# First batch of an attention and token-mixer kernel: v loaded as 128 rows, attention ahead of the token products

## The chip, the cores and the metric

The kernel runs on one core of a Trainium2 chip. A core has five engines, each with its own instruction queue that runs in order: TensorE (PE, matrix products, with PEld for the loading of its weights), VectorE (DVE), ScalarE (ACT), GpSimd (POOL) and SyncE (SP), which here issues DMA transfers. The engines wait for each other through semaphores. Data lies in DRAM, in SBUF (128 partitions) and in PSUM (banks of 128 partitions by 512 floats, into which PE writes). The metric is the device time of one execution in microseconds (us).

## The reference

Local attention with block summaries, followed by a token mixer and a channel mixer, all in float32. Batch 4, 8 heads, 768 positions, head dimension 64.

```python
k_sum = k.reshape(B, H, nb, 32, D).max(axis=3)       # nb = 24 blocks
v_sum = v.reshape(B, H, nb, 32, D).mean(axis=3)
scores_l = q @ k.T / sqrt(D)      # kept where |i - j| < 16
scores_s = q @ k_sum.T / sqrt(D) + log(32)
a = softmax([scores_l, scores_s]);  out = a @ [v, v_sum]
...
x = out as (batch, 768, 512)
h = relu(x.T @ w_tok1) @ w_tok2;  u = x + h.T         # token mixer, 256 hidden
y = u + relu(u @ w_ch1) @ w_ch2                       # channel mixer, 1536 hidden
```

## The kernel before

Heads are worked on in pairs, 4 pairs a batch (the text counts pairs 0 to 3 of batch 0). Positions are cut into 12 windows of 64 queries; each sees 96 keys (64 and 16 on either side) and the 24 block summaries, so 120 columns. For that the host lays out k and v as overlapping windows: `kw` holds the 96 keys of each window with room for the 24 summaries, `vw[b, h]` is 96 rows by 12 windows by 64.

Work on one pair of batch 0 runs through these steps. SP loads k, q and the v of two heads (`load_k`, `load_q`, `load_v`). DVE takes the maximum over key blocks and copies it beside the keys (`key_blocks`, L345 and L354). PE computes scores in two groups of windows (`scores`, L462, tiles `sc`), DVE adds the mask and takes the row minimum (L476), ACT takes the exponential (L486, tiles `e`). PE computes the block means of v (`first_means`, L374, tile `vm`), which DVE copies (L394) and POOL spreads into the last 24 rows of the v tile (L381). POOL also copies the raw v into its tile (L320). PE transposes `e` (`turn`, L524, tiles `et`), ACT evacuates that (L535, `eT`), PE computes the weighted sums (`weighted`, L594, `av`), and DVE normalises them into `x` (L602 to L614).

The token products follow: `tok1` (L748) multiplies x of one pair by w_tok1, ACT and DVE split the result in two parts (L729, L734); `tok2` (L828 and L836, tiles `up`) multiplies that by w_tok2 and adds the transposed x, in two halves of the positions (0 and 1), and ACT and DVE split it into `u`. Then come the channel products: for each of 12 slices f of the hidden layer `ch1` (L897, tiles `hp`) and `ch2` (L940, tiles `acc`).

The weights arrive as 64-bit words and are made into floats by `w_tick(i)`: tick 0 to 2 for w_tok1, 3 to 5 for w_tok2, 6 to 29 for the channel weights (tick 10 for the first product of slice 2). One tick is two loads, two ACT steps (L1466, L1472), one POOL step (L1479), two DVE steps (L1484, L1491) and, from tick 3 on, a split on ACT and POOL (L1511, L1517). The second ACT step writes a scratch tile `wp`, which the DVE steps read beside another tile.

What sets the order: nothing is issued where it is written. `add` records each piece of work with its engine, an estimated duration, its reads and writes and a rank; at the end `Plan.write` runs a list scheduler (`_order`), which simulates engines and DMA with the numbers in the code, takes ready work by rank (R_H first, then R_EVAC, R_ATT, R_LATER, R_W, R_BACK) and then by order of recording, and writes each engine's instructions in the order found. The engines then run them in that order, whatever the real times are. A buffer is a slot of a tag: the n-th slot of a tag with m buffers waits for the last user of slot n - m. PSUM banks have the tags mm and att (two banks each) and acc0 to acc3 (one each).

At the start PE does 21 warm-up products on zeros (L1530), while the first k and q are loaded. In batch 0 loads, attention and token products are recorded mixed, in the order of a list `FIRST`. The v tiles of the other batches are loaded as 96 rows as well, and their products are spread among the channel products of the batch before.

Of the kernel before, what the change touches and what calls it, by code (L numbers as in the profile page):

```python
# [76 lines left out]
class Plan:  # L77
    LATE = {"pe": 0.3, "act": 0.15, "dve": 0.15, "pool": 0.2, "sp": 0.0}
    RATE, FIRST, LAND, LANES = 250.0, 370.0, 2.1, 8

# [45 lines left out]
    def _order(self):  # L126
# [10 lines left out]
        queues = {e: [] for e in self.LATE}  # L137
        events, done, dma, lanes = [], [], 0.0, [0.0] * self.LANES

# [63 lines left out]
def tile_attention_mixer(  # L203
# [22 lines left out]
    def sbuf(shape, tag, name, bufs, dtype=F32):  # L226
        return plan.slot(sb, shape, dtype, tag, name, bufs)
# [19 lines left out]
    early = {n: sbuf([P, NT, D], "w2", f"vw_{n}", NF) for n in range(H)}  # L247
    early_k = sbuf([P, NT, NC], "x", "k_2", 2)
    w1_t = [sbuf([P, 2, NC4, P], "w1", f"w1_{f}", NF, F32R) for f in range(NF)]
    w2_t = [sbuf([P, 2, DM], "w2", f"w2_{f}", NF, F32R) for f in range(NF)]  # L250
# [9 lines left out]
        "start": ["att", "att", "acc0", "acc1"],  # L260
        "turned": ["mm", "mm"],
        0: ["att"],
# [13 lines left out]

    def tok_bank(name, late):
        if state["phase"] == "start":
            return bank(name, ["acc0", "acc1", "att", "att"] if late else ["acc3"])
        return bank(name, BANKS[state["phase"]])  # L280
# [13 lines left out]
    def load_q(p):  # L294
        b, hp = divmod(p, NP)
        q_t[p] = sbuf([P, S], "q", f"q_{p}", 2)
        return load(q_t[p], lambda t: t, q[b, hp], 393)
# [6 lines left out]
    def load_v(n):  # L304
# [7 lines left out]
        if b == 0:  # L312
            raw = early[n]
            load(raw, lambda t: t[:WIN], vw[b, h], 295)
            add(
                "pool", 0.1, lambda: nc.gpsimd.memset(slot.t[:NC, :, D:], 1.0),
                writes=[(slot, 2)], rank=R_ATT,
            )
            add(
                "pool", 0.85, lambda: nc.gpsimd.tensor_copy(slot.t[:WIN, :, :D], raw.t[:WIN]),  # L320
                reads=[(raw, 0)], writes=[(slot, 0)], rank=R_ATT,
            )
            return
# [112 lines left out]
    def scores(p, g, behind=()):  # L436
# [53 lines left out]

        for i in range(TT // 2):
            for j in range(2):
                n = 2 * p + j
                den, T = den_t[n], TT // 2 * g + i
                add(
                    "dve", 0.21, lambda n=n, j=j, i=i: lowest(n, j, i), reads=[(tiles[j], 0), ("mask", 0)],
                    writes=[(e, (j, i)), (den, ("min", T))], rank=R_ATT,
                )
                add(
                    "act", 0.39 if p >= NP else 0.29, lambda n=n, j=j, i=i: power(n, j, i), reads=[(den, ("min", T))],  # L500
                    writes=[(e, (j, i)), (den, ("sum", T))], rank=R_ATT,
                )
# [238 lines left out]
    def tok1(b, p):  # L741
        x2, a = x_t[b, p]
        pt = vm_bank

        def products():
# [9 lines left out]
            "pe", 2.8, products, reads=x_keys(b, p) + [(wt1, i) for i in range(3)],  # L755
            writes=[(pt, "t")], rank=R_ATT,
        )
        split_t1(
            b, p, lambda: pt.t[:, :DTOK].rearrange("p (k c) -> p k c", k=2), (pt, "t"), 0.39
        )  # L760
# [662 lines left out]
    def w_tick(i, behind=()):  # L1423
# [12 lines left out]
        for j in range(2):  # L1436
# [91 lines left out]
    def warm_up():  # L1528
        for _ in range(21):
            nc.tensor.matmul(pw.t, lhsT=warm.t[:, :P], rhs=warm.t, start=True, stop=True)  # L1530
# [6 lines left out]
    )  # L1537
    load_v(0)
    load_v(1)
    load_k(1)  # L1540
    load_q(1)
    load_v(2)
    load_v(3)
    load_k(2)
    key_blocks(0)

    tick = 0
    TICKS = {2: 3, 5: 6, 12: 7, 16: 8}
    for s in range(STEPS):
        att_step(0, s)  # L1550
        if s == 1:
            load_q(2)
        while tick < TICKS.get(s, 0):
            w_tick(tick)
            tick += 1
        if s == 1:
            load_v(4)
            load_v(5)
        if s == 4:
            load_k(3)  # L1560
            load_q(3)
        if s == 5:
            load_v(6)
            load_v(7)
        if FIRST[s][0] == "a":
            p = FIRST[s][1]
            tok1(0, p)
            if p:
                tok2(0, 0, p - 1)
    tok2(0, 0, NP - 1)  # L1570
    while tick < 10:
# [149 lines left out]
```

## Time and profile before

| | us |
|---|---|
| median of 3 runs | 568.28 (567.77 to 569.28) |
| the profiled execution | 566.26 |
| its span, first to last instruction | 564.2 |
| PE busy / DVE / ACT / POOL | 548.9 / 335.4 / 267.9 / 263.8 |
| start of the first channel product | 68.75 |
| mean granted PE clock | 0.994 of full speed |

The profile shows one execution. A row of the timeline gives start, duration, engine, source line, operation, output <- inputs, shape and count; in square brackets the idle time ahead of it and what ended it. A row of the waits gives who waited for whom, the total, how often, and the longest. A row of stretches gives the busy time of each engine in that stretch, the granted PE clock, the mean busy share of the 16 DMA engines and the rate that they moved. Busy PE time includes the pipelined end of a product, so the pitch from one start to the next is what a product costs.

### The profile page before, as it was taken

The page shows a single profiled execution, that of the slowest core. Times are in us where ns is not written, and L with a number is a line of the kernel's source. Part 1 is how long each engine was busy: PE and PEld are TensorE (multiplying, and loading weights), DVE is VectorE, ACT ScalarE, POOL GpSimd, SP SyncE. Part 2 cuts the span into 40 slices and gives each one's busy share as a digit, 9 for nine tenths or more (in the row PEclk, how much of TensorE's full clock was granted, in tenths as well). Part 3 has the DMA queues.
Part 4 walks back from the last instruction along what each step waited for, and adds up shares of the span by engine and source line. Part 5 has one row for each costly group of instructions (what it writes and reads, how often), then busy time and mean ns, then how long its engine had stood idle before and what let it go on. Part 6 is the DMA issues. An engine that isn't in the chain of part 4 may idle for free.

```text
span 564.2 us, 12750 instructions
## 1 busy us (share of the span) xinstructions
PE 548.9 (97%) x4629; PEld 485.7 (86%) x4629; DVE 335.4 (59%) x949; ACT 267.9 (47%) x771; POOL 263.8 (47%) x344
## 2 busy tenths in 40 slices
PE   8769999999999999999999999999999999999997
PEld 4658988878989988878799997887789999999997
DVE  4775677866573336456463436445352494899974
ACT  3668698765574334232242314242234253567642
POOL 1653387851133310158896511049879612444111
PEclk9889999999999999999999999999999999999999
DMA  8964478673755017768795606677788673543621
GB/s 268 341 176 130 130 238 264 200 227 106 219 177 177 26 38 198 188 188 231 224 246 174 130 11 192 147 186 211 188 246 241 181 256 116 193 139 95 198 94 65
DMA packets 133774, 99.52 MB, mean 176 GB/s; under 512 B 88272, under 2 KB 112464, under 8 KB 133712
## 3 DMA queue, kind: packets, MB, share of 16 engines
q1 hardware_dynamic: 133568, 98.52, 59.2%
q8 instruction: 36, 0.59, 0.4%
q14 instruction: 26, 0.21, 0.1%
q10 hardware_dynamic: 144, 0.20, 0.1%
HBM read 68.60 MB, written 28.31 MB: 172 GB/s over the span
## 4 chain that ended last, share of the span: by engine, by line
PE 87%; DMA 7%; DVE 2%; ACT 2%; issue 1%; ACTq 0%; DVEq 0%
PE acc L940 26%; PE hp L897 26%; PE up L836 6%; PE t1q L795 5%; PE av L594 4%; DMA vw<-in_vw 3%; PE sc L462 3%; PE pb L1170 3%; PE pa L1170 2%; PE qb L1170 2%; PE qc L1170 2%; PE pc L1170 2%; DMA w<-in_w_tok 2%; PE vm L748 2%; DMA vb<-in_vb 1%; PE qa L1170 1%
## 5 line engine op out<-in xcount | busy, mean ns | idle before, releaser
L940 PE MATMUL acc<-h,w 128*128 128x512 f32 (+1 forms) x864 | 164.0, 339 | 0.0
L897 PE MATMUL hp<-u,w 128*128 128x512 f32 (+1 forms) x864 | 161.8, 337 | 0.0
L897 PEld LDWEIGHTS hp<-u,w 128*128 128x128 f32 x864 | 133.3, 188 | 18.5 <-issue 1.4
L940 PEld LDWEIGHTS acc<-h,w 128*128 128x128 f32 x864 | 132.4, 188 | 19.1 <-ACT h L909 1.4
L486 ACT ACTIVATE e<-e,den 128x120 f32<-128x120 f32 x192 | 70.3, 386 | 53.0 <-DVE den L476 46.0
L909 ACT ACTIVATE h<-hp 128x512 fp32r<-128x512 f32 (+1 forms) x72 | 35.2, 489 | 117.7 <-PE hp L897 116.8
L914 DVE SCALAR_TENSOR_TENSOR h<-hp,h 128x512 fp32r<-128x512 f32 (+1 forms) x72 | 39.8, 553 | 75.1 <-ACT h L909 75.1
L1017 POOL TENSOR_TENSOR s<-s,w 128x256 f32<-128x256 f32 x84 | 62.2, 746 | 5.1
L979 POOL TENSOR_TENSOR ot<-ot,u 128x512 f32<-128x512 f32 (+1 forms) x24 | 23.7, 1014 | 57.5 <-DVE ot L971 27.7
L476 DVE CUSTOM_DVE_ANT_0 e<-sc,mask_sb 128x120 f32<-128x120 f32 x192 | 41.3, 277 | 15.0 <-PE sc L462 12.1
L1517 POOL TENSOR_TENSOR w<-wb,w 128x256 fp32r<-128x256 f32 x48 | 34.6, 740 | 17.0 <-ACT w L1511 16.7
L836 PE MATMUL up<-wt,t 128*128 128x512 f32 (+2 forms) x192 | 39.1, 344 | 0.0
L781 POOL TENSOR_TENSOR xs<-x,xs 128x512 fp32r<-128x512 f32 x18 | 23.2, 1291 | 21.3 <-ACT xs L776 21.3
L445 POOL MEMSET e<- 128x48 f32 x16 | 2.2, 138 | 65.9 <-DMA away<-e 19.6
L836 PEld LDWEIGHTS up<-wt,t 128*128 128x128 f32 x192 | 30.5, 189 | 2.5
L462 PEld LDWEIGHTS sc<-k,q 64*64 64x64 f32 x768 | 20.3, 135 | 12.0 <-issue 8.8
L462 PE MATMUL sc<-k,q 64*64 64x120 f32 x768 | 27.5, 275 | 3.1 <-DMA w<-in_w_tok 1.9
L594 PEld LDWEIGHTS av<-v,eT 120*64 120x64 f32 x768 | 23.9, 138 | 5.5 <-issue 3.1
L795 PE MATMUL t1q<-xs,ws 128*128 128x256 f32 x216 | 28.5, 283 | 0.0
L418 DVE TENSOR_REDUCE vs<-vb 96x8 f32<-96x256 f32 (+1 forms) x40 | 18.2, 458 | 16.8 <-DMA vb<-in_vb 16.7
L345 DVE TENSOR_REDUCE ks<-k 128x24 f32<-128x768 f32 x16 | 15.2, 947 | 21.3 <-DMA k<-in_kw 21.3
L594 PE MATMUL av<-v,eT 120*64 120x64 f32 (+1 forms) x768 | 26.1, 224 | 1.3 <-ACT eT L535 1.2
(128 smaller groups left out, 881.1 us busy)
## 6 DMA issues: line engine op xcount, KB each, us to landing
w<-in_w_ch SPq DMA_DIRECT2D x48, 256.0 KB
k<-in_kw SPq DMA_DIRECT2D x16, 720.0 KB
v<-in_vw SPq DMA_DIRECT2D x24, 288.0 KB
q<-in_q SPq DMA_DIRECT2D x16, 384.0 KB
away<-e SPq DMA_DIRECT2D x16, 384.0 KB
eT<-away SPq DMA_DIRECT2D x64, 96.0 KB
sums<-s SPq DMA_DIRECT2D x24, 256.0 KB
w2d<-w SPq DMA_DIRECT2D x12, 512.0 KB
```

What stands on the lines that cost most here:

```text
L462: nc.tensor.matmul(tiles[j].t[c * QT : (c + 1) * QT, i * NC : (i + 1) * NC], lhsT=qt.t[rows, t * QT : (t + 1) * QT], rhs=kt.t[rows, t, :], ...
L476: nc.vector.tensor_tensor_reduce(out=e.t[:, j, i * P : i * P + NC], in0=tiles[j].t[:, i * NC : (i + 1) * NC], in1=mask_sb[:, mv, :], op0=A ...
L486: nc.scalar.activation(ei, ei, AF.Exp, bias=den_t[n].t[:, 1, T : T + 1], scale=-1.0, accum_out=den_t[n].t[:, 0, T : T + 1] if p >= NP else ...
L594: nc.tensor.matmul(pv[cs, T], lhsT=eT[:NC, T % (TT // 2), cs], rhs=v.t[:NC, 2 * T + c], start=True, stop=True,)
L795: nc.tensor.matmul(pt.t[:, 2 * P * k : 2 * P * (k + 1)], lhsT=ws[:, wp, T, ks], rhs=xs[:, xp, T], start=(c == 0 and k == 0 and T == 0 and ...
L836: nc.tensor.matmul(pt.t[:, :nt], lhsT=t1.t[:, part, ks], rhs=wt2[w].t[:, k, h0 : h0 + nt], start=(far and k == 0 and i == 0), stop=(k == D ...
L897: nc.tensor.matmul(pt.t[:, :nt], lhsT=w1_t[f].t[:, w, c], rhs=us[c].t[:, part], start=(i == 0), stop=(i == len(ops) - 1),)
L909: lambda: nc.scalar.activation(h.t[:, 0], pt.t[:, :nt], AF.Relu),
L914: lambda: nc.vector.scalar_tensor_tensor(out=h.t[:, 1], in0=pt.t[:, :nt], scalar=0.0, in1=h.t[:, 0].bitcast(F32), op0=ALU.max, op1=ALU.sub ...
L940: nc.tensor.matmul(slot.t[:, c0 : c0 + nt], lhsT=w2_t[f].t[:, w, o * P : (o + 1) * P], rhs=h.t[:, part], start=(f == 0 and w == 0 and part ...
L1017: nc.gpsimd.tensor_tensor(out=out_, in0=left, in1=right, op=op)
L1170: nc.tensor.matmul(bank_.t[:, :HS], lhsT=w(i), rhs=x(j), start=first and n == 0, stop=True, skip_group_check=True,)
```

## The change

All of it concerns batch 0. (1) The raw v of a head is loaded as 128 rows instead of 96: the 96 rows of the head and the first 32 of the next one, which nobody reads. The load is of 393 kB instead of 295. (2) The loads come in the order of the pairs, and the weights behind them; q of pairs 2 and 3 gets buffers of its own (tag w1), so that it waits for none. (3) All attention of batch 0 is recorded ahead of the token products, and w_tok1's ticks have the rank of attention, w_tok2's a lower one. (4) Banks: transposes and weighted sums take mm, mm and acc3, the first token products acc0 and acc1 in turn instead of one bank, the second ones att, att and acc2. The scratch tile `wp` of ticks 0 to 5 moves from PSUM (acc3) to SBUF (tag q). (5) 17 warm-up products instead of 21. (6) Within a group of scores all three tiles of one head come ahead of those of the other. (7) The planner's DMA rate and start, and some paddings between slots (`APART`), have other numbers.

```diff
-    RATE, FIRST, LAND, LANES = 250.0, 370.0, 2.1, 8
+    RATE, FIRST, LAND, LANES = 250.0, 390.0, 2.1, 8
...
+    early_q = {p: sbuf([P, S], "w1", f"q_{p}", NF) for p in (2, 3)}
...
-        "turned": ["mm", "mm"],
+        "turned": ["mm", "mm", "acc3"],
...
-    def tok_bank(name, late):
+    def tok_bank(name, first=False):
         if state["phase"] == "start":
-            return bank(name, ["acc0", "acc1", "att", "att"] if late else ["acc3"])
+            return bank(name, ["acc0", "acc1"] if first else ["att", "att", "acc2"])
...
-            load(raw, lambda t: t[:WIN], vw[b, h], 295)
+            rows = vw.rearrange("b h w t d -> (b h w) t d")[WIN * n : WIN * n + P]
+            load(raw, lambda t: t, rows, 393)
...
-        for i in range(TT // 2):
-            for j in range(2):
+        parts = [(j, i) for j in range(2) for i in range(TT // 2)]
+        if p >= NP:
+            parts.sort(key=lambda x: x[1])
+        for j, i in parts:
...
-        pt = vm_bank
+        pt = tok_bank(f"t1p_{b}_{p}", True)
...
-    APART = {"u1": 32, "t1": 48, "w1": 16}
+    APART = {"u1": 32, "u0": 16, "ot": 32, "t1": 32, "w1": 16}
...
-        first, rank = two[0][2] is None, R_ATT if i < 6 else R_W
+        first, rank = two[0][2] is None, R_ATT if i < 3 else R_LATER if i < 6 else R_W
...
-        pb = bank(f"wp_{i}", ["acc3"] if i < 6 else ["acc0", "acc1"] if i < 10 else ["att"])
+        if i < 6:
+            pb = sbuf([P, 512], "q", f"wp_{i}", 2)
+        else:
+            pb = bank(f"wp_{i}", ["acc3"] if i < 10 else ["att"])
...
-        for _ in range(21):
+        for _ in range(17):
...
+    for p in range(NP):
+        if p:
+            load_k(p)
+            load_q(p)
+        load_v(2 * p)
+        load_v(2 * p + 1)
     key_blocks(0)
...
+    for tick in range(6):
+        w_tick(tick)
     for s in range(STEPS):
         att_step(0, s)
...
+    for tick in range(6, 10):
+        w_tick(tick)
+    tick = 10
+    for p in range(NP):
+        tok1(0, p)
+    for p in range(NP):
+        tok2(0, 0, p)
```

The loads on SP, from pair 2's k on. Before (line numbers of the kernel before; a number behind a name only tells tiles of one name apart):

```order
L290 DMA k_127<-in_kw 128x1440
L290 DMA vw_130<-in_vw 96x768
L290 DMA vw_132<-in_vw 96x768
L1440 DMA w_135<-in_w_tok 128x512 x2
L290 DMA q_203<-in_q 128x768
L1440 DMA w_211<-in_w_tok 128x512 x2
L1440 DMA w_251<-in_w_tok 128x512 x2
L290 DMA k_311<-in_kw 128x1440
L1440 DMA w_336<-in_w_tok 128x512 x2
L290 DMA q_374<-in_q 128x768
L290 DMA vw_402<-in_vw 96x768
L290 DMA vw_418<-in_vw 96x768
```

Of the change:

```order
L291 DMA k_123<-in_kw 128x1440
L291 DMA q_127<-in_q 128x768
L291 DMA vw_143<-in_vw 128x768
L291 DMA vw_163<-in_vw 128x768
L291 DMA k_200<-in_kw 128x1440
L291 DMA q_226<-in_q 128x768
L291 DMA vw_242<-in_vw 128x768
L291 DMA vw_263<-in_vw 128x768
L1444 DMA w_287<-in_w_tok 128x512 x2
L1444 DMA w_356<-in_w_tok 128x512 x2
L1444 DMA w_411<-in_w_tok 128x512 x2
```

Eight loads of token weights (w_tok1 and the first of w_tok2) stood ahead of the last two v; now all of attention's loads stand ahead of the first.

ACT, in the changed kernel, between the exponentials of pair 2 (the second group, `e_1_491`) and those of pair 3 (`e_0_583`); `wt_551` is w_tok1, and w_287, w_356 and w_411 are the three pairs of loads of ticks 0, 1 and 2:

```order
L488 ACTIVATE e_1_491<-e_1_491,den_431 128x120 x3
L1473 ACTIVATE wt_551<-w_287 128x512
L1479 ACTIVATE wp_571<-w_287 128x512
L539 ACTIVATE eT_0_577<-et_0_547 120x384
L1473 ACTIVATE wt_551<-w_356 128x512
L539 ACTIVATE eT_0_600<-et_0_579 120x384
L539 ACTIVATE eT_1_619<-et_1_588 120x384
L539 ACTIVATE eT_1_621<-et_1_596 120x384
L1479 ACTIVATE wp_649<-w_356 128x512
L1473 ACTIVATE wt_551<-w_411 128x512
L1479 ACTIVATE wp_662<-w_411 128x512
L488 ACTIVATE e_0_583<-e_0_583,den_584 128x120 x3
```

Before, at the same place (pair 2's second group is `e_1_355`, pair 3's first `e_0_450`, w_tok1 `wt_357`):

```order
L1466 ACTIVATE wt_357<-w_211 128x512
L535 ACTIVATE eT_0_453<-et_0_413 120x384
L486 ACTIVATE e_1_355<-e_1_355,den_287 128x120
L1466 ACTIVATE wt_357<-w_251 128x512
L486 ACTIVATE e_1_355<-e_1_355,den_284 128x120
L486 ACTIVATE e_1_355<-e_1_355,den_287 128x120
L535 ACTIVATE eT_0_487<-et_0_463 120x384
L1472 ACTIVATE wp_499<-w_211 128x512
L486 ACTIVATE e_0_450<-e_0_450,den_451 128x120
```

The steps on w_tok1 were spread among pair 2's exponentials, and the last of them came behind the first of pair 3; now all six stand between pair 2 and pair 3.

PE, in the changed kernel, from pair 2's weighted sums (`av_684`) through the last token product of the first kind, the identity transposes of a second token product and the matmuls of pair 0's:

```order
L598 MATMUL av_684<-v_408,eT_1_621 64x65 x6
L528 MATMUL et_0_706<-identf,e_0_583 120x128 x3
L528 MATMUL et_0_727<-identf,e_0_583 120x128 x3
L752 MATMUL t1p_0_744<-x_0_379,wt_551 128x128 x12
L528 MATMUL et_1_771<-identf,e_1_654 120x128 x3
L528 MATMUL et_1_779<-identf,e_1_654 120x128 x3
L752 MATMUL t1p_1_785<-x_0_379,wt_551 128x128 x12
L598 MATMUL av_817<-v_545,eT_0_722 64x65 x6
...
L598 MATMUL av_834<-v_574,eT_1_800 64x65 x6
L752 MATMUL t1p_2_850<-x_1_717,wt_551 128x128 x12
L752 MATMUL t1p_3_875<-x_1_717,wt_551 128x128 x12
L832 MATMUL up_0_0_908<-identf,x_0_379 128x128 x4
```

Before, the stretch behind pair 2's weighted sums held one more pair's sums of v, both score groups of pair 3 and the first two second token products between these steps; now scores and sums of pair 3 lie ahead of it, the four first token products stand close together, and the second ones follow behind all attention. The token products of pairs 2 and 3 in the second half (`up_1_2`, `up_1_3`), which stood ahead of the first channel product, now follow behind it.

More of the change, by code (lines that the diff above doesn't have):

```diff
@@ L137, in _order @@
         queues = {e: [] for e in self.LATE}
-        events, done, dma, lanes = [], [], 0.0, [0.0] * self.LANES
+        events, done, dma, lanes = [], [], 0.95, [0.0] * self.LANES
         def release(w):
@@ L295, in load_q @@
         b, hp = divmod(p, NP)
-        q_t[p] = sbuf([P, S], "q", f"q_{p}", 2)
+        q_t[p] = early_q[p] if p in early_q else sbuf([P, S], "q", f"q_{p}", 2)
         return load(q_t[p], lambda t: t, q[b, hp], 393)
@@ L755, in tok1 @@
             "pe", 2.8, products, reads=x_keys(b, p) + [(wt1, i) for i in range(3)],
-            writes=[(pt, "t")], rank=R_ATT,
+            writes=[(pt, 0)], rank=R_ATT,
         )
         split_t1(
-            b, p, lambda: pt.t[:, :DTOK].rearrange("p (k c) -> p k c", k=2), (pt, "t"), 0.39
+            b, p, lambda: pt.t[:, :DTOK].rearrange("p (k c) -> p k c", k=2), (pt, 0), 0.39
         )
@@ L816, in tok2 @@
         h0, nt = H0[b][half], HT[b][half]
-        pt = tok_bank(f"up_{b}_{half}_{p}", p >= NP - 2)
+        pt = tok_bank(f"up_{b}_{half}_{p}")
         tag, bufs, whole = f"u{half}", 4, b == B - 1
@@ L1528, in warm_up @@
     def warm_up():
-        for _ in range(21):
+        for _ in range(17):
             nc.tensor.matmul(pw.t, lhsT=warm.t[:, :P], rhs=warm.t, start=True, stop=True)
-    add("pe", 7.0, warm_up, reads=[(warm, 0)], writes=[(pw, 0)])
+    add("pe", 5.2, warm_up, reads=[(warm, 0)], writes=[(pw, 0)])
     load_k(0)
@@ L1537, in tile_attention_mixer @@
     )
[L1538 to L1544, printed above, removed]
+    for p in range(NP):
[4 more added lines that the diff above has]
+        load_v(2 * p + 1)
     key_blocks(0)
-    tick = 0
-    TICKS = {2: 3, 5: 6, 12: 7, 16: 8}
+    for tick in range(6):
+        w_tick(tick)
     for s in range(STEPS):
         att_step(0, s)
[L1551 to L1571, printed above, removed]
-        w_tick(tick)
-        tick += 1
+    for tick in range(6, 10):
+        w_tick(tick)
+    tick = 10
[3 more added lines that the diff above has]
+        tok2(0, 0, p)
     start = [sum(HT[0][j // NF] // 256 for j in range(i)) for i in range(2 * NF + 1)]
```

## The prediction

> **What bounds the kernel now.** The page comes first, then busy time by stretch: the first 69 us against what follows.
>
> ```profile
> span 564.2 us, 12750 instructions
> ## 1 busy us (share of the span) xinstructions
> PE 548.9 (97%) x4629; PEld 485.7 (86%) x4629; DVE 335.4 (59%) x949; ACT 267.9 (47%) x771; POOL 263.8 (47%) x344
> ...
> core 0: us, PE busy (x) PEld busy (x) DVE busy (x) ACT busy (x) POOL busy (x), PEclk, DMA share, GB/s
> 0.00:69.00 69.00, 58.33 (x815) 47.81 (x816) 42.31 (x169) 42.66 (x112) 29.61 (x54) 0.95 0.67 208
> 69.00:120.00 51.00, 51.00 (x224) 41.86 (x223) 40.15 (x70) 42.68 (x104) 39.25 (x59) 1.00 0.76 242
> ```
>
> TensorE (PE) is the bound: from 69 us it has no gap for 51 us, and of 15.3 us without PE work in the whole span 10.7 lie in the first 69. All that the diff touches lies there too: the attention and token products of batch 0, up to the first channel product. Call that product's start T0. The order of PE's matmuls behind it is the same before and after, but for two token products (pairs 2 and 3, second half) that now stand behind T0, and one exchange among the first channel products. So the question is how much earlier PE gets through this work. Which waits does it have there? The waits of PE, 0 to 75 us:
>
> ```profile
> PE vm L374 <- DMA vw<-in_vw: 3.9, 3, 2.1
> PE sc L462 <- DMA w<-in_w_tok: 1.9, 1, 1.9
> ...
> PE sc L462 <- DMA q<-in_q: 1.2, 1, 1.2
> ```
>
> 7.0 us of the idle time are loads. The chain of waits says the same of the first 34 us:
>
> ```profile
> 0.74 4.25 DMA k<-in_kw
> ...
> 5.01 10.15 DMA vw<-in_vw
> ...
> 15.18 9.71 DMA w<-in_w_tok
> ...
> 24.91 9.30 DMA vw<-in_vw
> ```
>
> It consists of transfers alone. The last v lands at 34.2, because eight token-weight loads (262 kB each) are queued ahead of it. The gaps cost twice, as the granted clock shows (columns: stretch, length, PE busy, PEclk, DMA share, GB/s):
>
> ```profile
> 15.75:18.55 2.80, 2.80 (x40) 0.50 1.04 234
> 36.00:39.60 3.60, 3.60 (x36) 0.53 0.17 59
> ```
>
> Each group of gaps is followed by about 3 us at half clock, about half of it lost: 1.4 and 1.7 us.
>
> **The loads.** The same view by stretch of transfer, the first with 128-row loads only, the second while the last two 96-row v are on their way:
>
> ```profile
> 21.00:28.00 7.00, 1.00 1.04 395
> ...
> 28.50:32.00 3.50, 1.00 1.05 238
> ```
>
> A 96-row v of 295 kB at 238 takes 1.24 us, one of 393 kB at 395 takes 1.00. So the eight wider loads carry 0.79 MB more and still save 1.9 us; from the two rates the ends against before are +3.3 us (393 kB at 238, 1.65 each) and -1.9, and I take -1.9, since q, of the same row length, goes by in the first stretch. The first k (737 kB) lands at 5.0; from there at 395 kB a us the last v (7.85 MB in all) lands at 23.0, and the third pair of w_tok1 loads (9.42 MB) at 27.0. That is 11 us earlier for v.
>
> [...]
>
> **PE's own work up to T0**, from its timeline:
>
> ```profile
> 1.19 6.70 PE L1530 MATMUL warm<-warm 128*128 128x512 f16 x21 [1.19 <-DVE warm L1525]
> 7.82 1.46 PE L462 MATMUL sc<-k,q 64*64 64x120 f32 x48
> ...
> 24.57 1.53 PE L374 MATMUL vm<-vw,means 96*24 96x64 f32 x48
> ...
> 50.17 0.82 PE L524 MATMUL et<-identf,e 128*120 128x128 f32 x6
> ...
> 51.71 2.94 PE L748 MATMUL vm<-x,wt 128*128 128x128 f32 x24
> 54.49 0.82 PE L524 MATMUL et<-identf,e 128*120 128x128 f32 x6
> ...
> 57.07 1.62 PE L594 MATMUL av<-v,eT 120*64 120x65 f32 x48
> 58.62 0.66 PE L828 MATMUL up<-identf,x 128*128 128x128 f32 x4
> ...
> 60.52 0.38 PE L828 MATMUL up<-identf,x 128*128 128x128 f32 x2
> ...
> 61.45 2.84 PE L748 MATMUL vm<-x,wt 128*128 128x128 f32 x24
> ...
> 65.06 0.38 PE L828 MATMUL up<-identf,x 128*128 128x128 f32 x2
> ...
> 68.75 5.65 PE L897 MATMUL hp<-u,w 128*128 128x512 f32 x24
> ```
>
> From start to start: a first token product 2.78 (51.71 to 54.49), a pair's weighted sum 1.55, a second token product 1.90 (first half) or 0.93 (second half), six transposes 0.8, a pair's scores 1.5, its v sums 1.5. The four warm-ups taken out stood last, at some 0.22 each; the first scores followed them at once, so the gain is between 0 and 0.9. I take 0.9 (scores from 6.95), as q, 393 kB behind k, should be there at about 6.0.
>
> After the loads, VectorE (DVE) and ScalarE (ACT) set the pace of attention. DVE normalises a head in 0.89 (22.17 to 23.06), takes a masked minimum in 0.20, a key maximum in 0.95; ACT does six exponentials in 1.8 and a weight step in 0.6:
>
> ```profile
> 22.17 0.16 DVE L602 TENSOR_SCALAR rec<-av 128x6 f32<-128x6 f32 x1
> ...
> 23.06 0.15 DVE L602 TENSOR_SCALAR rec<-av 128x6 f32<-128x6 f32 x1
> ...
> 23.95 0.27 DVE L476 CUSTOM_DVE_ANT_0 e<-sc,mask_sb 128x120 f32<-128x120 f32 x1
> ...
> 24.15 0.28 DVE L476 CUSTOM_DVE_ANT_0 e<-sc,mask_sb 128x120 f32<-128x120 f32 x1
> ...
> 28.02 0.95 DVE L345 TENSOR_REDUCE ks<-k 128x24 f32<-128x768 f32 x1 [0.41 <-DMA k<-in_kw]
> ...
> 27.80 0.66 ACT L1472 ACTIVATE wp<-w 128x512 int32<-128x512 uint32 x1
> ...
> 43.82 1.82 ACT L486 ACTIVATE e<-e,den 128x120 f32<-128x120 f32 x6
> ```
>
> I walked the four queues of the changed kernel by hand with these. Pair 0: scores to 8.4, sums to 10.7 (they wait for v). Pair 1: q at 11.4, scores to 13.6, sums to 15.5. DVE has 12 minima, a maximum with its copy, two sum copies and two heads a pair, about 6 us, and holds PE there: pair 2's scores end at 20.7, pair 3's at 27.0, the weighted sum of pair 2 at 30.1. ACT meanwhile has two steps for each of three pairs of w_tok1 loads ahead of pair 3's exponentials; the third pair of loads is there at 27.0, its first step comes up at 29.4, its second is through at 30.5. The first token product waits for DVE's last step on the third w_tok1 piece, which stands behind two heads of pair 2: 34.0. From there PE has its inputs early: 4 x 2.78 + 0.8 + 1.55 + 4 x 1.90 + 2 x 0.93 = 22.9, so T0 = 56.9. The second token products need w_tok2's last piece, some 46 by the same walk, and start at 47.5: hidden, and 1.4 us of slack; beyond it each us counts.
>
> **Terms that the trace doesn't show.** (a) The clock: from 30.1 to 34.0 PE has only 0.8 us of work, like the two stretches above; one half-clock stretch, 0 to 1.7, I take 1.7. (b) The pieces of w_tok1 and w_tok2 pass through SBUF instead of a PSUM bank, so twelve DVE steps now read SBUF twice:
>
> ```profile
> L1484 DVE SCALAR_TENSOR_TENSOR wp<-wb,wp x27: 682/695/697, 36.7 to 119.6; 128x512 int32<-128x512 int32 x27
> ...
> L1019 DVE SCALAR_TENSOR_TENSOR rs<-rs x12: 677/688/1217, 495.1 to 536.1; 128x512 fp32r<-128x512 f32 x12
> ```
>
> With one operand in PSUM 27 of them all took 0.68 to 0.70; the same size with both in SBUF took up to 1.22. Six are ahead of the first token product: 0 to 6 x 0.53 = 3.2, while GpSimd (POOL) copies v and spreads means most of that time. I take 0.3 each, 1.8.
>
> [...]
>
> (c) The channel weights. Tick 10 fills a slot that the x of pairs 0 and 1 leaves:
>
> ```profile
> 74.06 1.45 POOL L1517 TENSOR_TENSOR w<-wb,w 128x256 fp32r<-128x256 f32 x2
> ...
> 77.00 2.89 PE L897 MATMUL hp<-u,w 128*128 128x512 f32 x12
> ```
>
> Free at 65.06, ready at 75.5: 10.4 us, needed at 77.0. Now it is needed 2.73 + 1.86 + 2.73 + 2.76 = 10.1 behind T0 (2.73 and 2.76 are a channel group's pitch): a stall of 0.3 to 0.4, which I add. (d) q, banks and slot paddings: no instruction more, none taken away on a waiting engine; 0.
>
> **Sum.** T0 = 56.9 + 1.7 + 1.8 = 60.4, and 1.9 of token products and 0.4 of stall come behind it: 62.7 against 68.75, a gain of 6.1. The profiled execution took 566.26 (span 564.2): 560.2. Its median of runs is 568.28, 2.0 above; on that scale **562.2**.
>
> **Rivals.**
> [...]
> - *v comes no faster a byte* (0.17): at 238 the eight v take 5.2 us more than I reckon, the third w_tok1 piece lands at 32.2 instead of being waited for at 29.4, and 2.8 us are added: 565.0. Were all loads at the pace at which they landed before (9.16 MB at 34.2, 288 GB/s from 5.0 on), it lands at 35.2, 5.8 added: 568.0, no change. Against: the 395 of seven us.
> - *The gain is given back to the weights* (0.09): if the preparation of channel weights does not move with T0, PE can gain only the 1.5 us between 75.5 and 77.0: 566.8. Against: the slot's release moves with PE, and ACT is 62% busy before T0.
> - *Slower* (0.07): ACT works in order, and its steps on w_tok1 now stand ahead of pair 3's exponentials. From a landing of the third piece at 35.5 on (285 GB/s from 5.0 on) that wait eats all 6.1. At 238 throughout it lands at 41.5, 12.1 added: 574.3. For it: 238 is measured; against: only beside 96-row loads.
>
> **Numbers.** The forecast, 559.5 to 564.5, gets 0.47. The range 557.0 to 567.0 leaves out the last rival, half of the 288 end and a little below the first: about 0.14. A measurement here can tell 0.3%, 1.7 us, from no change: faster 0.85 (forecast, first rival, most of the second, half of the third), same 0.09, slower 0.06.
>
> **What would show it.** The last v landing at 23 to 25, not 34; no wait of PE's sums for v after 10 us; 128-row loads near 395 GB/s up to 25; the first token product near 34 to 36, T0 at 59 to 61; one half-clock stretch behind 34 at most; some w_tok steps on DVE at 0.9 to 1.2; PE without gaps from T0 to 120. I am wrong if the third w_tok1 piece lands after 32, if ACT holds pair 3 for long, or if channel products wait for weights.

## The result, and the profile after

| | before | after |
|---|---|---|
| median (range) of 4 runs each, us | 568.02 (567.24 to 569.28) | 562.55 (561.48 to 563.80) |
| ratio after / before, 95% interval | | 0.9902 (0.9875 to 0.9930) |
| the profiled execution / its span | 566.26 / 564.2 | 563.80 / 561.4 |
| PE busy in the span | 548.9 | 546.0 |
| start of the first channel product | 68.75 | 62.90 |

The kernel is 5.5 us (1.0%) faster. The prediction said 562.2 with 557.0 to 567.0. The number fits; its terms do so only in part, and T0, at 62.90, lies outside the 59 to 61 that were named as a sign. First the loads, in the transfer view of the changed kernel for 0 to 48 us (40 slices of 1.2 us; busy tenths, then the rate):

```profile
DMA  0499989999999999999999984659898200006000
GB/s 0 101 379 385 300 326 415 398 411 410 447 397 402 417 434 400 393 395 389 388 391 389 375 310 147 213 162 367 278 318 331 94 0 0 0 3 205 11 0 0
```

From 7 us on the rate is about 400 without a dip to 238. Summed up (each slice times 1.2 us), 7.85 MB are through at 22.0 us and 9.42 MB at 26.0. That is not yet the landing: in the trace a load reports in 16 semaphore steps (those of the last v come from 21.8 to 23.8). By the last of them the last v landed at 23.8 and the third pair of w_tok1 loads at 28.1; the prediction had 23.0 and 27.0. SP's queue shows it too: it keeps eight loads under way, on eight semaphores in turn, so the eighth load behind the last v is issued when that v has landed.

```profile
23.80 0.33 SPq L1444 DMA_DIRECT2D w<-in_w_tok  x1
```

Then the waits of PE, 0 to 75 us:

```profile
PE t1p L752 <- DVE den L478: 3.1, 1, 3.1
PE sc L464 <- DVE k L356: 1.5, 1, 1.5
PE warm L1537 <- DVE warm L1532: 1.2, 1, 1.2
PE et L528 <- ACT eT L539: 0.8, 1, 0.8
PE vm L376 <- DMA vw<-in_vw: 0.6, 1, 0.6
```

Of 7.0 us of waits for loads 0.6 are left; the 1.5 for DVE's key maxima go back in part to a load as well, since DVE had waited 0.64 for pair 1's k. The largest wait is now one for DVE, ahead of the first token product. What that stretch looks like on PE (timeline of the changed kernel; the columns are those of before), and the clock in it:

```profile
28.02 1.02 PE L464 MATMUL sc<-k,q 64*64 64x120 f32 x24
28.96 1.53 PE L376 MATMUL vm<-vw,means 96*24 96x64 f32 x48
30.42 1.62 PE L598 MATMUL av<-v,eT 120*64 120x65 f32 x48
...
36.99 5.49 PE L752 MATMUL t1p<-x,wt 128*128 128x128 f32 x24 [3.12 <-DVE den L478]
```

```profile
0.00:69.00 69.00, 60.56 (x828) 50.62 (x829) 47.04 (x175) 46.21 (x121) 33.25 (x57) 0.95 0.65 233
...
36.00:37.00 1.00, 0.01 (x1) 0.01 (x1) 1.00 (x5) 0.03 (x1) 0.00 (x0) 0.53 0.93 348
37.00:42.00 5.00, 5.00 (x23) 5.00 (x24) 3.52 (x10) 3.06 (x8) 1.99 (x3) 0.50 0.09 32
```

PE has nothing to do for 3.1 us; then the first token product runs at half clock and takes 5.49 instead of the 2.84 that the second one needs. The mean clock of the first 69 us is 0.95, as before the change. So the loads came early, about as predicted, and part of their gain stayed in a new gap with its half clock.

One difference lies outside the start. The second channel products, in all four batches, cost less; these are the rows of the pages, before and after (total in us, mean of one in ns):

```profile
L940 PE MATMUL acc<-h,w 128*128 128x512 f32 (+1 forms) x864 | 164.0, 339 | 0.0
L897 PE MATMUL hp<-u,w 128*128 128x512 f32 (+1 forms) x864 | 161.8, 337 | 0.0
```

```profile
L944 PE MATMUL acc<-h,w 128*128 128x512 f32 (+1 forms) x864 | 162.3, 337 | 0.0
L901 PE MATMUL hp<-u,w 128*128 128x512 f32 (+1 forms) x864 | 161.6, 336 | 0.0
```

Together that is 1.9 us, and the second traces of both kernels (e10 and e11 below) show the same: 323.9 instead of 325.7. The work is the same and the clock from 69 to 555 us is 1.00 in all four traces. No run here shows the cause. The experiments ask what the width and the order of the loads are worth, and what makes the gap.

### The profile page after: what moved, and what is told of

The parts are those of the page before. It is cut to its first block, busy times and chain, and to the rows that moved or that the text cites. A ratio compares the mean times of both kernels' runs of the same rounds, so it can differ in the third digit from the quotient of the medians.

```text
span 561.4 us, 12755 instructions
## 1 busy us (share of the span) xinstructions
PE 546.0 (97%) x4625; PEld 484.5 (86%) x4625; DVE 337.7 (60%) x949; ACT 267.9 (48%) x771; POOL 265.7 (47%) x344
## 4 chain that ended last, share of the span: by engine, by line
PE 84%; DMA 7%; DVE 4%; SPq 1%; ACT 1%; issue 1%; POOL 1%; ACTq 0%; DVEq 0%; POOLq 0%
PE hp L901 25%; PE acc L944 25%; PE up L840 6%; PE t1q L799 5%; PE av L598 3%; PE pb L1174 3%; PE sc L464 3%; PE t1p L752 2%; PE pa L1174 2%; PE qb L1174 2%; PE qc L1174 2%; PE pc L1174 2%; DMA vb<-in_vb 1%; DMA k<-in_kw 1%; PE et L528 1%; PE qa L1174 1%
## 5 line engine op out<-in xcount | busy, mean ns | idle before, releaser
L944 PE MATMUL acc<-h,w 128*128 128x512 f32 (+1 forms) x864 | 162.3, 337 | 0.0
L901 PE MATMUL hp<-u,w 128*128 128x512 f32 (+1 forms) x864 | 161.6, 336 | 0.0
L901 PEld LDWEIGHTS hp<-u,w 128*128 128x128 f32 x864 | 133.1, 188 | 18.2 <-issue 1.4
L464 PEld LDWEIGHTS sc<-k,q 64*64 64x64 f32 x768 | 19.9, 132 | 10.0 <-issue 9.2
L464 PE MATMUL sc<-k,q 64*64 64x120 f32 x768 | 26.8, 271 | 1.5 <-DVE k L356 1.5
L799 PEld LDWEIGHTS t1q<-xs,ws 128*128 128x128 f32 x216 | 27.0, 190 | 0.3
L488 ACT ACTIVATION_READ_ACCUMULATOR e<-e,den 128x1 f32 x144 | 27.1, 188 | 0.0
L598 PEld LDWEIGHTS av<-v,eT 120*64 120x64 f32 x768 | 23.8, 138 | 3.8 <-issue 2.4
```

Source lines behind the costliest of these rows:

```text
L464: nc.tensor.matmul(tiles[j].t[c * QT : (c + 1) * QT, i * NC : (i + 1) * NC], lhsT=qt.t[rows, t * QT : (t + 1) * QT], rhs=kt.t[rows, t, :], ...
L488: nc.scalar.activation(ei, ei, AF.Exp, bias=den_t[n].t[:, 1, T : T + 1], scale=-1.0, accum_out=den_t[n].t[:, 0, T : T + 1] if p >= NP else ...
L598: nc.tensor.matmul(pv[cs, T], lhsT=eT[:NC, T % (TT // 2), cs], rhs=v.t[:NC, 2 * T + c], start=True, stop=True,)
L799: nc.tensor.matmul(pt.t[:, 2 * P * k : 2 * P * (k + 1)], lhsT=ws[:, wp, T, ks], rhs=xs[:, xp, T], start=(c == 0 and k == 0 and T == 0 and ...
L901: nc.tensor.matmul(pt.t[:, :nt], lhsT=w1_t[f].t[:, w, c], rhs=us[c].t[:, part], start=(i == 0), stop=(i == len(ops) - 1),)
L944: nc.tensor.matmul(slot.t[:, c0 : c0 + nt], lhsT=w2_t[f].t[:, w, o * P : (o + 1) * P], rhs=h.t[:, part], start=(f == 0 and w == 0 and part ...
```

## Experiments

All ran five rounds unless said otherwise. Beside the median stand: the ratio to the kernel before on the same chip; T1, the start of the first channel product of 256 columns in the profiled execution (it stands behind the same products in all variants, unlike T0); and the half-clock loss, worked out for each execution as (1 - mean granted clock) x span and averaged. A half-clock stretch of 3.4 us loses 1.7. The loss counts every such stretch, wherever it lies.

| | median us | ratio (95%) | T1 | clock loss, us (executions) |
|---|---|---|---|---|
| before | 567.3 to 568.0 | 1 | 135.45; 133.82 | 4.0 (54) |
| after; e10, the same again | 562.55; 562.91 | 0.9902; 0.9915 (0.9892 to 0.9938) | 130.99; 130.79 | 3.1 (10) |
| e1 narrow v | 564.67 | 0.9951 (0.9926 to 0.9977) | 132.09 | 3.3 (12) |
| e2 before + wide v | 564.04 | 0.9932 (0.9909 to 0.9955) | 129.49 | 2.3 (9) |
| e3 21 warm-ups | 563.05 | 0.9912 (0.9882 to 0.9942) | 130.70 | 3.6 (6) |
| e4 large filler | 566.66 | 0.9983 (0.9958 to 1.0007) | 136.03 | 3.4 (12) |
| e5 wp in PSUM | 560.84 | 0.9874 (0.9833 to 0.9915) | 127.13 | 0.6 (6) |
| e6 small filler | 559.17 | 0.9850 (0.9808 to 0.9893) | 129.24 | 0.6 (6) |
| e7 split product | 561.44 | 0.9875 (0.9831 to 0.9919) | 127.51 | 0.7 (6) |
| e8 old load order | 570.15 | 1.0036 (1.0010 to 1.0063) | 134.59 | 4.4 (12) |
| e9 = e5 + e7 | 560.84 | 0.9874 (0.9843 to 0.9905) | 126.76 | 0.7 (5) |

**e1, the width undone.**

```diff
-            load(raw, lambda t: t, rows, 393)
+            load(raw, lambda t: t[:WIN], rows[:WIN], 393)
```

> The changed kernel with each of the eight v loads cut to its 96 useful rows again (295 kB in place of 393); the order on every engine is that of the changed kernel. Theory, as predicted: a 96-row v moves at 238 GB/s and takes 1.24 us where the wide one takes 1.00 at 395, so the last v lands 1.9 us later than with wide loads; the waits for v of pair 0 (0.63) and for k of pair 1 (1.48) grow by 0.5 each, T0 (62.90) moves to 63.4 to 64.8 and the time from 562.5 to 563.0 to 564.4. Rival, rows do not matter: 0.79 MB less at 395 GB/s, the last v 2.0 us earlier, T0 62.4 or earlier, time 562.0 or less. Second rival, loads no longer bound anything behind pair 0: T0 and time as with wide loads, within 0.3.

Measured: 564.67, 1.8 above e10, T1 1.1 to 1.3 later. The stretches of transfer, first the changed kernel, then e1 (the last three numbers: clock, DMA share, GB/s):

```profile
11.00:14.00 3.00, 1.52 (x29) 1.31 (x32) 2.25 (x4) 2.00 (x6) 1.54 (x2) 1.00 1.03 416
17.00:20.00 3.00, 2.69 (x75) 2.22 (x73) 2.77 (x11) 1.81 (x6) 2.20 (x5) 1.00 1.03 412
```

```profile
11.00:14.00 3.00, 1.63 (x30) 1.42 (x34) 2.24 (x4) 1.82 (x5) 1.10 (x2) 1.00 1.05 258
17.00:20.00 3.00, 2.24 (x52) 1.78 (x51) 1.79 (x4) 0.99 (x4) 0.61 (x1) 1.00 1.05 282
```

The DMA engines are busy all the same, but move 258 and 282 GB/s instead of 416 and 412. The theory holds, and the rival that rows do not matter falls. At 270, the mean of the two e1 rows, 295 kB take 1.09 us; 393 kB at 414 take 0.95: the wide load is no slower in spite of its extra bytes. (Parts of k and q pass in these stretches too.) The landing shows more: the eighth load behind the last v is issued at

```profile
28.86 0.78 SPq L1444 DMA_DIRECT2D w<-in_w_tok  x1
```

so the last v lands 5.0 later than in the changed kernel (28.8 against 23.8, and 23.9 in e10). The prediction had 1.9 for the width. The semaphore steps of this one load come over 4.1 us, those of the wide one over 2.0. Little of it reaches T1: in the changed kernel DVE is busy for 14.2 of the 15 us from 22 to 37 and sets the pace there; in e1 it is busy for 12.7 of them.

**e2, the width alone,** in the kernel before: `load(raw, lambda t: t, rows, 295)` with `rows` as in the change.

> The kernel before with one edit: the eight v loads take 128 rows (393 kB) instead of 96; all orders are those of the kernel before. Theory: each v takes 1.00 instead of 1.24 us, the last v lands 1.9 us earlier than 34.2, PE's waits for v (3.9 us) shrink by up to 1.9, and the time goes from 568.0 to 566.1 to 567.5. Rival, the width brings no faster byte: 393 kB at 238 are 1.65 us each, 3.3 us later, 570 to 571.3. Second rival: the order of the loads bounds, not the rate of the narrow ones; within 0.3 of before.

Measured: 564.04, 3.4 below the kernel before, twice what was expected. The rate of transfer from 0 to 48 us in slices of 1.2, of the kernel before and of e2, and e2's row to be set against 0.00:69.00 (clock 0.95) of before:

```profile
GB/s 0 91 374 384 286 290 278 320 395 279 265 245 353 280 220 219 329 385 387 407 389 401 403 303 239 234 263 308 370 359 143 36 0 0 0 0 0 0 0 0
```

```profile
GB/s 0 77 360 398 340 344 429 389 403 412 456 376 418 397 407 396 370 409 395 403 393 407 378 387 394 402 273 77 0 0 0 0 0 0 0 63 210 176 160 326
```

```profile
0.00:69.00 69.00, 60.88 (x841) 50.00 (x842) 46.58 (x177) 48.16 (x125) 33.23 (x60) 1.00 0.67 238
```

The dips, which in the kernel before stand where v is on its way, are gone, and by the semaphore steps the last v lands at 29.2 instead of 34.2 (33.5 in e11): 4 to 5 us, not 1.9. What had not been reckoned with either is the clock: with shorter waits for v this execution has no half-clock stretch up to 69 us, and on average the loss falls from 4.0 to 2.3. Half of the 3.4 us is clock.

So the width alone, in the old order, brings 3.4 us where the whole change brings 4.5 to 5.5. T1 is even earlier here (129.49) than in the changed kernel. Whether the rest of the change adds anything to the width is not settled: the medians say 1.1 to 1.5, and the intervals of the ratios overlap. The channel products alone could make that: they take 327.1 us in e2 and 323.9 in the changed kernel.

**e8, the order undone** (the first 25 loads issued in the order of the kernel before, all else of the change kept):

```diff
+        order = self._order()
+        sp = [i for i, w in enumerate(order) if w.eng == "sp"][:25]
+        loads = [order[i] for i in sp]
+        turn = [*range(10), 11, 12, 17, 18, 10, *range(19, 23), 13, 23, 24, 14, 15, 16]
+        for i, k in zip(sp, turn):
+            order[i] = loads[k]
```

> The changed kernel with its first 25 loads issued in the order of the kernel before: the wide v of pairs 2 and 3, k and q of pair 3 stand behind three to four pairs of w_tok1 and w_tok2 loads. The order on the other engines is that of the changed kernel. Theory: at some 400 GB/s the last v lands 5 us later (28 to 30 instead of 23 to 25), pair 3's scores and with them the token products come 2 to 5 later, T0 65 to 68, 564.5 to 567. Rival: with wide v the loads are fast enough in either order, and the order was worth nothing: T0 within 0.5, 562 to 563.

Measured: 570.15, slower than the kernel before, 7.2 above e10. The timeline of e8 shows the wait for q of pair 2 (its line number is that of L464; the wait is booked to the weights that land with it), and the stretch at half clock behind the gap:

```profile
20.64 1.02 PE L472 MATMUL sc<-k,q 64*64 64x120 f32 x24 [2.15 <-DMA w<-in_w_tok]
```

```profile
38.00:44.00 6.00, 4.16 (x19) 4.16 (x20) 4.48 (x16) 3.10 (x8) 2.46 (x4) 0.52 0.33 115
```

By the semaphore steps the last v lands at 29.0 instead of 23.8, as expected, and T0 is 65.41, 2.5 to 2.7 later, within the expected as well. The time is not: T1 is 3.6 to 3.8 later, and the rest comes behind it. There the page shows another row that differs, to be set against L901 of the changed kernel (161.6, 336):

```profile
L909 PE MATMUL hp<-u,w 128*128 128x512 f32 (+1 forms) x864 | 165.2, 341 | 0.0
```

The first channel products cost 3.6 us more over the whole kernel, the second ones 0.9 (163.2), at a granted clock of 1.00 from 69 us on. That makes 4.5 of the 8.4 us between the spans of e8 and e10 (568.1 and 559.7); 2.7 are T0. The edit moves loads of batch 0 alone, and ACT, DVE and POOL do their work in the same order in both; why the products of all batches are longer, no run shows. The order of the loads is thus worth 2.5 to 2.7 us in T0, with the rest of the change (attention first, banks) in place. That is still more than the 1.1 to 1.3 that the width is worth there (e1). What the order would be worth in the kernel before was not run.

**e3, the warm-ups:** `range(21)` for `range(17)`.

> The changed kernel with 21 warm-up products instead of 17, all orders the same otherwise. By the term of the prediction the first scores start 0.9 us later (7.9 instead of 7.00) and everything behind them too: T0 63.8, 563.4. Rival: the waits behind them, 0.63 us for v of pair 0 and 1.48 us for k of pair 1, take it up: scores 0.9 later, but T0 62.9 and 562.5 as before; then the four fewer warm-ups were worth nothing.

Measured: 563.05, T1 130.70: no difference. PE of e3:

```profile
7.64 1.46 PE L464 MATMUL sc<-k,q 64*64 64x120 f32 x48
...
13.41 1.46 PE L464 MATMUL sc<-k,q 64*64 64x120 f32 x48 [1.48 <-DVE k L356]
```

The first scores start 0.64 later than in the changed kernel (7.00), those of pair 1 at the same time (13.41 against 13.49): they wait for DVE's key maxima, which wait for k. The rival holds.

**e4, a filler in the gap,** to see whether the idle time makes the half clock:

```diff
+        def fill():
+            for _ in range(24):
+                nc.tensor.matmul(pt.t[:, :P], lhsT=identf, rhs=identf, start=True, stop=True)
...
+            add("pe", 0.0, fill, writes=[(pt, 0)], rank=R_ATT)
```

> The changed kernel with 24 products of the identity (128 columns each, some 2.8 us at full clock) ahead of the first token product, into the bank that this product overwrites; nothing else is changed, and the output is the same. Theory: TensorE ran at half clock from 36.0 to 42.6 because it stood idle for 3.1 us ahead; with the gap filled the first token product takes 2.84 instead of 5.49, T0 comes 2.5 to 3.0 earlier (60.0 to 60.4) and the time goes to 559.5 to 560.2. Rival: the clock falls because of the earlier gaps (11 to 25 us), whatever stands in the last one: half clock as before, 562.5, or some 1 us more if the filler then runs at half clock and ends after the third weight piece is ready. Second rival: TensorE comes earlier but then waits for the second token weights (ready at 47.4, needed at 50.2 then) or for the channel weights: less than 1 us won.

Measured: 566.66, 4 us slower. It failed by its own making, twice. PE and DVE of e4:

```profile
38.12 6.98 PE L751 MATMUL t1p<-identf 128*128 128x128 f32 x48 [3.10 <-DVE den L478]
```

```profile
37.19 0.68 DVE L1505 SCALAR_TENSOR_TENSOR wt<-w,wp 128x512 int32<-128x512 int32 x1
37.78 0.28 DVE L478 CUSTOM_DVE_ANT_0 e<-sc,mask_sb 128x120 f32<-128x120 f32 x1
```

A float product counts as two rows (x48 for 24), so the filler was twice as long as meant. And it did not run in the gap: it reads no weights, and still waited until 38.12, just behind a minimum of pair 3 (37.78 + 0.28 = 38.06). That shows a second wait that the change brings: the first token product now takes bank acc0, which a score tile of pair 3 holds until DVE has read it, and this minimum stands behind the last w_tok1 step (37.19) in DVE's queue.

**e6, the filler done right:** 12 products behind the last transposes ahead of the gap, into unused columns of bank acc2.

```diff
+                for _ in range(12 if (p, g, j) == (3, 0, 1) else 0):
+                    nc.tensor.matmul(vm_bank.t[:, :P], lhsT=identf, rhs=identf, start=True, stop=True)
```

> The changed kernel with 12 products of the identity (some 2.8 us at full clock, half the work of the filler in e4) behind the last transposes ahead of the first token product, into columns of bank acc2 that nobody reads; all other orders are the same and so is the output. They fit into TensorE's idle stretch of 3.1 us (33.9 to 37.0). Theory: without that stretch the clock stays up, the first token product takes 2.84 instead of 5.49, T0 comes at 60.0 to 60.5, the time falls by 1.5 to 2.7 to 559.8 to 561. Rival: the half clock comes from the gaps at 11 to 30 us and stays: T0 62.9 to 65, 562.5 to 564.5.

Measured: 559.17, the fastest of all, 3.7 below e10. PE of e6:

```profile
34.75 2.85 PE L533 MATMUL vm<-identf 128*128 128x128 f32 x24
38.06 2.94 PE L754 MATMUL t1p<-x,wt 128*128 128x128 f32 x24 [0.46 <-DVE den L478]
```

The token product starts no earlier, but takes 2.94 instead of 5.49. The clock loss falls from 3.1 to 0.6 on average. Work that is thrown away is the only difference (the order on DVE, ACT and POOL is the same), so the idle gap made the half clock behind it. It stands behind the gap in all five traces that keep one of 2.6 to 3.1 us there (the changed kernel, e10, e3, e4, e8), and in none of e5, e6, e7 and e9. Beyond its own length the gap cost about 3.0 us in the first trace and 1.5 in e10. The average of 2.5 can hold other stretches too: e10 has one at 13.9 to 17.3 us, ahead of the gap, and e6 keeps one at 13.6 to 17.0. The clock covers 2.5 of the 3.7 us; the rest is open. (The execution profiled here, 562.25, is the slowest of its six; T1 is 1.6 to 1.8 earlier.)

**e5, the scratch tile back in PSUM** (and the planner's order shifted a little by it):

```diff
-        "turned": ["mm", "mm", "acc3"],
+        "turned": ["mm", "mm"],
...
-        if i < 6:
-            pb = sbuf([P, 512], "q", f"wp_{i}", 2)
-        else:
-            pb = bank(f"wp_{i}", ["acc3"] if i < 10 else ["att"])
+        pb = bank(f"wp_{i}", ["acc3"] if i < 10 else ["att"])
```

> The changed kernel with the scratch wp of the first six token-weight pieces back in PSUM bank acc3 (one buffer), and acc3 taken from the transposes again; the planner puts a few steps of DVE in another place for it. Theory: with one operand in PSUM all twelve DVE steps take 0.68 to 0.70 and none 1.06 to 1.21, the last step ahead of the first token product ends up to 1.4 earlier, T0 goes from 62.9 to 61.5 and the time from 562.5 to 561.1. Rival: one bank in place of two buffers makes ScalarE wait for DVE, and the transposes wait for banks; T0 and time as before or up to 2 us later.

Measured: 560.84, 2.1 below e10; T1 3.7 to 3.9 earlier. The six DVE steps on w_tok1, in the timeline of the changed kernel and, grouped (shortest, median and longest in ns), in e5:

```profile
28.24 0.69 DVE L1491 SCALAR_TENSOR_TENSOR wp<-wt,wp 128x512 int32<-128x512 int32 x1 [0.16 <-POOL wt L1486]
28.97 1.20 DVE L1498 SCALAR_TENSOR_TENSOR wt<-w,wp 128x512 int32<-128x512 int32 x1
...
30.69 1.06 DVE L1491 SCALAR_TENSOR_TENSOR wp<-wt,wp 128x512 int32<-128x512 int32 x1
31.79 0.69 DVE L1498 SCALAR_TENSOR_TENSOR wt<-w,wp 128x512 int32<-128x512 int32 x1
...
33.03 1.21 DVE L1491 SCALAR_TENSOR_TENSOR wp<-wt,wp 128x512 int32<-128x512 int32 x1
...
36.05 0.68 DVE L1498 SCALAR_TENSOR_TENSOR wt<-w,wp 128x512 int32<-128x512 int32 x1
```

```profile
L1488 DVE SCALAR_TENSOR_TENSOR wp<-wt,wp x3: 685/687/695, 28.0 to 33.6; 128x512 int32<-128x512 int32 x3
L1495 DVE SCALAR_TENSOR_TENSOR wt<-w,wp x3: 679/686/687, 28.8 to 35.1; 128x512 int32<-128x512 int32 x3
```

In SBUF three of the six are stretched, by 0.51, 0.37 and 0.52, 1.40 together; in PSUM none. POOL was at work beside each of the three: with a copy of means (28.27 to 29.62), with two of its own steps on w_tok1 (29.70 to 31.21), with two copies of means (32.87 to 34.93). PE's single gap of 3.1 us has become three of 0.5, 0.6 and 1.0 in e5, and the half clock is gone as well (loss 0.6), so that T1 gains more than the 1.4 of the steps. The planner moved some steps too, so how much of it is the steps alone isn't told apart.

**e7, real work in the gap:** the first token product in bank acc2, cut by the three pieces of w_tok1, each cut with its own wait.

```diff
+        pt = vm_bank if p == 0 else tok_bank(f"t1p_{b}_{p}", True)
...
+            for i in range(3):
+                add(
+                    "pe", 0.95, lambda i=i: piece(i), reads=x_keys(b, p) + [(wt1, i)],
+                    writes=[key], rank=R_ATT,
+                )
```

> The changed kernel with the first token product in the free columns of bank acc2 (its bank before the change) and cut by the three pieces of w_tok1, so that the products of the pieces that are ready run in the idle stretch of 33 to 37 us. Theory: 1.9 us of its 2.84 move into the stretch, the clock stays up or loses less (up to 2.65), T0 comes at 58.5 to 61, the second token products start at 48.5 to 51, just behind their weights (47.4). Of 2 to 4.5 us won there about half is given back at 145 to 170 us, where TensorE waits for DVE in all the variants so far: 560 to 561.5. Rival: the weights of the second token product come later too, since ScalarE and DVE are full, and T0 gains less than 1: 562 or more.

Measured: 561.44, within the expected; T1 3.3 to 3.5 earlier. PE of e7:

```profile
32.91 1.16 PE L763 MATMUL vm<-x,wt 128*128 128x128 f32 x8 [0.72 <-DVE vs L396]
33.90 0.49 PE L528 MATMUL et<-identf,e 128*120 128x128 f32 x3
34.23 1.06 PE L763 MATMUL vm<-x,wt 128*128 128x128 f32 x8
36.64 1.16 PE L763 MATMUL vm<-x,wt 128*128 128x128 f32 x8 [1.36 <-DVE wt L1516]
...
46.77 2.94 PE L752 MATMUL t1p<-x,wt 128*128 128x128 f32 x24 [1.41 <-DVE x L618]
```

Two thirds of the product run in the gap and just ahead of it, the clock holds, and 1.41 us come back as a wait for DVE's normalisation of pair 3. (The planner moved a few steps of DVE, ACT and POOL here too.)

**e9, e5 and e7 together.**

> The edits of e5 and e7 together: the scratch wp of the first six pieces in PSUM bank acc3, and the first token product in bank acc2, cut by the pieces of w_tok1. Theory: the DVE steps take 0.69, the last w_tok1 piece is ready at 35.8 as in e5, two thirds of the first token product are done by then, and the first half of the second token products starts 1 to 2 us ahead of e5 (49.2): 558.5 to 560. Rival: what follows is held by DVE's normalisation of pair 3, which e7 showed as a wait of 1.4 ahead of the last token product, so that nothing is won over e5: 560.5 to 561.5.

Measured: 560.84; T1 126.76, 0.4 ahead of e5, but no better in the median. The rival holds (a wait of 1.2 for the normalisation of pair 3 is left). e5, e6, e7 and e9 are each 1.5 to 3.7 below the changed kernel in the median. All their intervals overlap with its own, so their order among each other is not settled; that they lose less clock is (0.6 to 0.7 in 23 executions against 3.1 in 10).

**e10 and e11, the two kernels again** (e11 for a trace only).

> The changed kernel as it is, once more, as the base for the variants. Theory: the half clock behind TensorE's idle stretch comes and goes between executions in whole stretches (1.7 us lost each); 562.5 in the median, spans of 559 to 562, mean granted clock 0.994 to 0.997. The trace again has TensorE idle for some 3 us ahead of the first token product, and some 2 us idle at 145 to 170 us, as in all variants. Rival: the idle time at 145 to 170 us was of that one execution, and is 0.5 as before the change.

> The kernel before, as it is, for a second trace: the one at hand was 1.8 us under its median. Theory: the other executions lose more at 145 to 170 us (1.5 to 2.5 idle instead of 0.5), and the same 4 us by waits for v and q up to 69 us; first channel product at 68 to 69.5. Rival: they lose it to a further half-clock stretch up to 69 us, and the first channel product comes at 70 or later.

Measured: 562.91 for the changed kernel, 566.02 and a span of 564.0 for the execution of before, which again lies below the median of its kernel. Its T0 is 67.13, earlier than both the theory and the rival had it; its idle time at 145 to 170 us, 1.6, is as the theory had it. The stretch 145 to 170, first of the first trace of the changed kernel, then of e10, then of e11 (the second number is PE's busy time, of 25.00):

```profile
145.00:170.00 25.00, 22.44 (x328) 20.79 (x327) 13.93 (x72) 15.29 (x64) 5.06 (x4) 1.00 0.56 168
```

```profile
145.00:170.00 25.00, 24.08 (x346) 22.31 (x346) 14.51 (x73) 16.12 (x65) 5.18 (x5) 1.00 0.60 184
```

```profile
145.00:170.00 25.00, 23.36 (x334) 21.70 (x334) 14.53 (x74) 16.73 (x68) 5.04 (x4) 1.00 0.61 178
```

Idle 2.6, 0.9 and 1.6, and 0.5 in the first trace of before. So the 2 us that the first trace of the changed kernel seemed to give back there belong to that execution, not to the change. In e10 the first token product starts at 38.21, takes 4.35, and T0 is 62.71.

## Why the prediction was right, and where not

- **The loads: right, but the width was put too low.** Last v landed at 23.8 (23.0 predicted), third w_tok1 pair at 28.1 (27.0), at a rate of 388 to 447. The width was reckoned at 1.9 us of landing, from the rates of whole stretches; the last v lands 5.0 later without it in e1, and 4 to 5 earlier with it in e2. In time that is 1.8 in e1 and 3.4 in e2. The second rival (no faster a byte) is out. In e1 the DMA share is 1.05, as high as with wide loads (1.03), at 258 and 282 GB/s instead of 416 and 412: how busy the engines are does not give the rate.
- **The warm-ups: wrong.** The 0.9 was 0 (e3). The walk itself had the scores of pair 1 wait for their loads, so a gain ahead of them could not reach T0.
- **The start of the first token product: 36.99 and 38.21, predicted 34.0 and 1.8 for the DVE steps that read SBUF twice, 35.8.** The 1.8 was the author's estimate between 0 and 3.2, from steps of 677 to 1217 ns before. It was near: 1.40 measured, as three of the six steps took 0.51, 0.37 and 0.52 more, each beside work of POOL. By what mechanism, no run shows. So 34.0 plus 1.4 leaves 1.6 to the walk, which was too fast: it had pair 3's scores end at 27.0, and their second half started at 28.02. And term (d), "banks: 0", missed that bank acc0 is held by pair 3's minima; in the changed kernel this is worth 0.2 (the minimum ends at 36.93, the weight step at 36.73), so it was wrong in kind and small in size.
- **The clock: right in kind, its size changes.** 1.7 was taken; 2.65 (5.49 instead of 2.84) and some 0.3 more on the next transposes were lost behind the gap in the first trace, 1.5 in e10. e6 shows the cause. T0 came at 62.90: 60.4 plus 1.2 (start) plus 1.25 (clock). In e10 it came at 62.71, with a start 2.4 later than predicted.
- **Stall of 0.4 at tick 10: none.** The first product of slice 2 starts at 73.02 without idle time ahead of it, and PE is dense from T0 to 120. The rival that gives the gain to the channel weights is out.
- **The number: by luck.** T0 came 2.3 to 2.5 us later than predicted, which alone would make 564.5 to 564.7. Against it stand the stall of 0.4 that did not come and 1.9 of shorter channel products. The prediction took the products as unchanged, since PE's order behind T0 is nearly the same before and after; the same order did not cost the same time. The base was uncertain by as much. The prediction added 2.0 from the profiled execution to the median. For before that held; the first profiled execution of the changed kernel lies 1.25 above its median. Over 54 and 10 executions the spans' medians are 565.6 and 560.8: a gain of 4.8, where 6.1 was forecast.
- **Rivals.** The first of them has the walk alone, without the terms for the clock and the DVE steps: T0 at 56.9, a gain of 9.6, 558.7. It did not happen, but e6 (559.17) is close to it: it was the price of the gap. "Slower" did not happen. e8 is slower than the kernel before, by a ratio of 1.0036, but its late loads account for 2.5 to 2.7 us only; less the 4.5 of longer channel products its median would lie below that of the kernel before.

## What to carry to other kernels

Where loads bound the start, order them by need and give them all 128 rows, even at the price of bytes that nobody reads: here the width, one line, brought 3.4 us in the old kernel, and with all else of the change in place the order was worth 2.5 to 2.7 in T0. Try the small edit alone first: what the rest adds to it could not be told from nothing. Then look at what the freed time turns into: a gap of 3 us on TensorE cost 1.5 to 3.0 us more through the clock, and filling it, even with waste, brought 3.7 in the median. Compare the same work far from the change as well: products that nobody touched were 1.9 us shorter here and 4.5 longer in e8. Before a scratch tile goes from PSUM to SBUF, look at what GpSimd does at that time: here three of six DVE steps took 0.37 to 0.52 longer beside its work.

## What the runs showed of the hardware

- The half clock comes in whole stretches: the mean clocks of the executions cluster near 1.000, 0.997, 0.994 and 0.991 of some 561 us, steps of 1.7 us. In the kernel before they range from 0.988 to 1.000 over 54 executions. They explain a quarter of the spread of its spans (correlation 0.49); the rest is elsewhere and open. In the 13 traces every half-clock stretch, but for those at the very end of the span, lasts 3.4 or 6.8 us. Gaps of 2.6 (e10) and 3.1 us ahead of the first token product were followed by it. In e2 a gap of 1.8 at 150.3 us was followed by half clock too, while one of 2.4 at 18.3 was not, so the length alone does not decide.
- A 96-row load kept the DMA engines as busy as a 128-row one (1.05 and 1.03) at 258 to 282 GB/s instead of 412 to 416, and the last of them landed 5.0 us later.
- The stretching of DVE steps that read SBUF twice is the same in three traces to 0.01 us (the changed kernel, e10, e3: 1.20, 1.06, 1.21). In e1, with the same order on both engines but later loads, the second to fifth step took 1.20, 0.69, 0.98 and 1.21 instead of 1.20, 1.06, 0.69 and 1.21, so the order alone does not decide which steps are stretched; in the changed kernel each stretched step had POOL at work beside it. POOL pays as well: in the changed kernel its copy of means that started 0.03 behind a DVE step took 1.35 (28.27), where the one at 24.93, with no such step beside it, took 0.83.
- The same 1728 channel products took 323.9 us in the two traces of the changed kernel, 325.7 and 325.8 in those of the kernel before, 327.1 in e2 and 328.4 in e8. The cause is open.
